# Float64 weights of a Hyena-and-two-MLP kernel: all decoded during the convolution, with four VectorE instructions a job

## The chip, the cores and the metric

One core of one Trainium2 chip runs the whole kernel. The time is device microseconds of one execution. The core has TensorE (PE in the profile, PEld for its weight loads), VectorE (DVE), ScalarE (ACT), GpSimd (POOL) and SyncE (SP, which here only issues DMAs). Three runs of the kernel before have a median of 3026.67 us.

## The reference, cut to what matters

```python
# x, v: (2, 12480, 128); pos_emb: (12480, 64)
h_filt = (np.maximum(pos_emb @ w1, 0.0) @ w2) * np.exp(-0.01 * pos)[:, None]
u = x * v
y = irfft(rfft(u, n=2*S, axis=1) * rfft(h_filt, n=2*S, axis=0), n=2*S, axis=1)[:, :S]
x = (x * y).reshape(24960, 128)
for each of two layers:                      # w_in (128, 2048), w_out (2048, 128), float64
    h = x @ w_in
    g = h if h > 0 else exp(h) - 1           # first layer
    g = h * cos(h)                           # second layer
    x = g @ w_out
```

The four weight matrices arrive as float64, since a float32 array is multiplied there by a float64 scalar. The chip gets them as 64-bit integers and has to make float32 values of them, with all 24 bits of mantissa and a split in two parts: a rounded one (`hi`, float32r) and the rest (`lo`).

## The kernel before, in words

**Filter (0 to about 50 us).** The taps of the filter are computed into `h_all`.

**Convolution (about 50 to 740 us).** 32 chunks of four channels go through a transform in stages: `st_a` (matmuls into `ps_a`, two multiplications by twiddle factors `za` and `zb` on VectorE, their sum `z_t` on POOL), `st_b` (matmuls into `ps_b`, and the product with the filter `ya`, `ps_b`, `y_t` on VectorE, rounded to `yh` on ACT), `lo_y` (`yl = y_t - yh` on POOL), `st_c` (matmuls into `ps_c`, `wa` and `wb` on VectorE, the sum `w_t` on POOL) and `st_d` (matmuls into `ps_d`, `at` on VectorE, a DMA to `xt_d`). `prod` multiplies x and v on POOL (`u_t`). For each chunk `k` is 0 and 1 for the two sequences and 2 for the filter; with k = 2, `st_b` only evacuates, on ACT (`hr`, `hi_f`, lines 360 to 362). The accumulators `ps_a`, `ps_b` and `ps_c` have one buffer each, so the next matmuls into one wait for the VectorE instructions that read it. The order of all this is the list `steps`, written out by hand and run 34 times; one run of the list is called a pass here, and each engine executes its instructions in the order in which the list emits them. All loads of x and v, all stores and the decoder's transfers are on SP's one queue.

**First decoder.** `Decode` is a generator: it emits a few instructions, yields, and is resumed by `next(now, None)` in the loop over `steps`, after every `st_a`, `st_c`, `st_d` and `lo_y` from the second pass on. That makes nine slots a pass. A job takes 256 columns (or rows) of one matrix: `words` (lines 112 to 123) takes the upper and the lower 32-bit words apart, `split` (125 to 145) makes the value `av` and the rest `bv`, `store` (147 to 167) writes `hi` and `lo` to `w_d` in HBM, and for two of the eight blocks of w_out the unsplit value to `wf_d`. Six instructions of a job are VectorE's: `sg`, `mag`, `keep`, `bits`, `av`, `pw`. POOL has `bv`, `dv` and `lo`, ACT has `sq`, `lf` and the copy to `hi`. A job takes nine yields, one more where `wf_d` is written. This generator does the 16 jobs of the first layer.

**Layers (about 740 us to the end).** Each of 52 tiles of 480 tokens per layer runs through eight blocks (`gemm1`, the nonlinearity, a split, `gemm2` five blocks later); line 578 copies the finished tile of the first layer into `x1`.

**Second decoder.** `arena` decodes the second layer's weights during the first layer, in eight jobs of 512 columns, in the part of `x1` that is still free. One `next(later, None)` per block advances it, from block 8 on. Here `dv` and `lo` are VectorE's too (`self.e`), eight VectorE instructions a job. The weights are read back from `w_d` at the end of the first layer (`reload`).

Of the kernel before, what the change touches and what calls it, by code (L numbers as in the profile page):

```python
# [18 lines left out]
B, S, D, FO, DFF = 2, 12480, 128, 64, 2048  # L19
# [10 lines left out]
T = 480  # L30
# [10 lines left out]

DELAY = (1, 2)
DELAY_A = (2, 2)
TINY = float(np.array([897 << 20], np.int32).view(np.float32)[0])


def tables():
# [27 lines left out]
def hyena_moe_kernel(ctx: ExitStack, tc: tile.TileContext, x, v, pe, w1, w2,  # L75
                     wi1, wo1, wi2, wo2, fa, tw, dft, ti, g, win, out):
    nc = tc.nc
# [18 lines left out]
    class Decode:  # L96


        def __init__(self, alloc, n, layer, which, q):
            self.t, self.layer, self.which, self.n = alloc, layer, which, n  # L100
            self.e = nc.vector if layer else nc.gpsimd
            self.o = o = q * n
            w = ((wi1, wo1), (wi2, wo2))[layer][which]
            self.wide = w.dtype != F32
            self.raw = self.t("raw", w.dtype)
            if which == 0:
                nc.sync.dma_start(self.raw, w[:, o:o + n])
            else:
                nc.sync.dma_start(self.raw.rearrange("p (k d) -> p k d", d=128),
                                  w[o:o + n, :].rearrange("(k p) d -> p k d", p=128))  # L110

        def words(self):
            if not self.wide:
                return
            w = self.raw.bitcast(I32).rearrange("p (n w) -> p n w", w=2)
            top, low = w[:, :, 1], w[:, :, 0]
            self.sq, self.lf, self.sg, self.mag = self.t("sq", F32), self.t("lf", F32), self.t("sg", I32), self.t("mag", I32)
            nc.scalar.activation(self.sq, top.bitcast(F32), AF.Square)
            nc.vector.tensor_scalar(self.sg, top, -2147483648, None, op0=ALU.bitwise_and)
            yield  # L120
            nc.scalar.activation(self.lf, low.bitcast(U32), AF.Copy, scale=2.0 ** -52)
            nc.vector.tensor_scalar(self.mag, top, 3, 0x7FFFFFFF, op0=ALU.logical_shift_left, op1=ALU.bitwise_and)
            yield

        def split(self):
            self.hi, self.lo = self.t("hi", F32R), self.t("lo", F32R)
            if not self.wide:
                self.av = self.raw
                copy_r(self.hi, self.raw)
                yield  # L130
                return
            keep, bits, self.av, pw, self.bv = (self.t("keep", I32), self.t("bits", I32), self.t("av", F32),
                                                self.t("pw", I32), self.t("bv", F32))
            nc.vector.tensor_scalar(keep, self.sq, TINY * TINY, -1.0, op0=ALU.is_ge, op1=ALU.mult)
            yield
            nc.vector.scalar_tensor_tensor(bits, self.mag, 0x40000000, self.sg,
                                           op0=ALU.bitwise_xor, op1=ALU.bitwise_or)
            yield
            nc.vector.tensor_tensor(self.av.bitcast(I32), bits, keep, op=ALU.bitwise_and)  # L139
            yield  # L140
            nc.vector.tensor_scalar(pw, self.av.bitcast(I32), -8388608, None, op0=ALU.bitwise_and)
            copy_r(self.hi, self.av)
            yield
            nc.gpsimd.tensor_tensor(self.bv, self.lf, pw.bitcast(F32), op=ALU.mult)
            yield

        def store(self):
            l, wh, n, p = self.layer, self.which, self.n, self.o
            nc.sync.dma_start(w_d[l, wh, 0, :, p:p + n], self.hi.bitcast(F32))
            for m in FULL[l] if wh else ():  # L150
                o = m * 256 - p
                if 0 <= o < n:
                    full = self.av[:, o:o + 256]
                    if self.wide:
                        full = self.t("full", F32)[:, 0:256]
                        nc.gpsimd.tensor_tensor(full, self.av[:, o:o + 256], self.bv[:, o:o + 256], op=ALU.add)
                        yield
                    nc.sync.dma_start(wf_d[l, m], full)
            if self.wide:
                dv = self.t("dv", F32)  # L160
                self.e.tensor_tensor(dv, self.av, self.hi.bitcast(F32), op=ALU.subtract)
                yield
                self.e.tensor_tensor(self.lo, dv, self.bv, op=ALU.add)
            else:
                nc.gpsimd.tensor_tensor(self.lo, self.av, self.hi.bitcast(F32), op=ALU.subtract)
            yield
            nc.sync.dma_start(w_d[l, wh, 1, :, p:p + n], self.lo.bitcast(F32))

        def run(self):
            for part in (self.words, self.split, self.store):  # L170
                yield from part()

    with tc.manual_schedule():
        with ExitStack() as cs:
            taps_ = cs.enter_context(tc.tile_pool(name="taps", bufs=1))
            const = cs.enter_context(tc.tile_pool(name="const", bufs=1))
# [23 lines left out]
            with ExitStack() as fs:  # L200
# [3 lines left out]
                pw = fs.enter_context(tc.tile_pool(name="pw", bufs=1, space=PSUM))  # L204
# [102 lines left out]
            with ExitStack() as vs:  # L307
# [102 lines left out]
                def alloc(name, dt):  # L410
                    return (p2 if name == "raw" else p1).tile([128, 256], dt, name=name, tag=f"d_{name}")

                def first_layer():
                    jobs = [(0, w, q) for w in range(2) for q in range(DFF // 256)]
                    nxt = Decode(alloc, 256, *jobs[0])
                    for i in range(len(jobs)):
                        dec = nxt
                        if i + 1 < len(jobs):
                            nxt = Decode(alloc, 256, *jobs[i + 1])
                        yield from dec.run()  # L420

                now = first_layer()
                prod(0, 0)
                steps = ((st_a, 0, 2), (st_b, 1, 1), (lo_y, 1, 0), (st_d, 2, 1), (prod, 0, 1), (st_a, 0, 0),
                         (lo_y, 1, 1), (prod, -1, 0), (st_c, 1, 0), (st_b, 0, 2), (st_a, 0, 1),
# [1 line left out]
                for p in range(NCH + 2):  # L427
                    for f, back, k in steps:
                        if 0 <= p - back < NCH:
                            f(p - back, k)  # L430
                        if f in (st_a, st_c, st_d, lo_y) and p > 0:
                            next(now, None)
                        if f is prod and back < 0:
                            load(p + 2)
# [149 lines left out]
        def reload(n, wh):  # L584
            l, j, m = blocks[n]
            if l == 0 and j == NTC - 1:
                layers[1].load(nc.sync, wh, m)

        ARENA = T * 20
        ASIZE = (B * S - ARENA) // 2  # L590

        def arena():
            jobs = [(1, w, q) for w in range(2) for q in range(DFF // 512)]
            for i, job in enumerate(jobs):
                free = [ARENA + i % 2 * ASIZE]

                def alloc(name, dt):
                    n = 512 * (2 if name == "raw" and dt != F32 else 1)
                    t = x1[:, free[0]:free[0] + n]
                    free[0] += n  # L600
                    return t if dt == F32 else t.bitcast(dt)

                dec = Decode(alloc, 512, *job)
                for _ in range(4):
                    yield
                yield from dec.run()

        later = arena()
        for wh in range(2):
            for q in range(NBLK):  # L610
                layers[0].load(nc.scalar, wh, q)
# [8 lines left out]
        for n in range(NBK + LAG):  # L620
            if n < NBK:
                l, j, m = blocks[n]
                gemm1(n)
                reload(n, 0)
                if 8 <= n < 200:
                    next(later, None)
                if m == NBLK // 2:
                    nl, nj = (l, j + 1) if j + 1 < NTC else (l + 1, 0)
                    if nl < 2:
                        split_x(nl, nj)  # L630
                    if l == 0:
# [46 lines left out]
```

## Time and profile before

| | us |
|---|---|
| median of three runs | 3026.67 (3023.61 to 3031.22) |
| profiled execution, its own time | 3032.04 |
| span of the profile | 3030.2 |
| granted TensorE clock over the span | 0.993 |

The 1.8 us between the profiled execution's time and its span lie around the program. The profiled execution is 5.4 us above the median of the runs. In the rows below L12 is line 12 of the kernel, `out<-in` are the program's names without buffer numbers (tiles of the arena are all called `x`), and an arrow `<-` behind a wait names what ended it.

### The profile page before, as it was taken

To read this page: it belongs to the slowest core of one execution; us is meant where nothing else is said; L and a number is where in the kernel's file an instruction comes from. 1 tells how busy PE (TensorE), PEld (TensorE's weight loads), DVE (VectorE), ACT (ScalarE), POOL (GpSimd) and SP (SyncE) were. 2 spreads that over 40 slices of the span, in tenths; PEclk is the share of its full clock that TensorE was granted. 3 is DMA by queue.
4 is the path that set the end of the run, shared out by engine and by line. 5 is a ranking of instruction groups with operands and counts; after the bars stand their busy time and mean duration, and the time that the engine had idled before them with its cause. 6 is when DMAs were issued, how large, how long until landed. Compare 5 with 4: busy or idle time off the path is not lost.

```text
span 3030.2 us, 38341 instructions
## 1 busy us (share of the span) xinstructions
PE 2966.4 (98%) x13140; PEld 2317.9 (76%) x13140; DVE 2587.9 (85%) x3272; ACT 2006.6 (66%) x3076; POOL 2575.1 (85%) x1632
## 2 busy tenths in 40 slices
PE   8999999998999999999999999999999999999999
PEld 6777677775777777888888887787888878888887
DVE  5999987876999998888888888788888888888887
ACT  2111111112887888888888888788888888888887
POOL 4888877775898998888888888888888888888888
PEclk9999999998999999999999999999999999999999
DMA  3232322222011100000000001000000000000000
GB/s 103 76 84 78 87 63 64 63 53 88 24 38 38 45 21 10 14 10 14 10 14 11 14 11 40 23 14 10 14 11 13 11 14 10 14 11 14 11 14 14
DMA packets 79635, 96.16 MB, mean 32 GB/s; under 512 B 5722, under 2 KB 63096, under 8 KB 79442
## 3 DMA queue, kind: packets, MB, share of 16 engines
q1 hardware_dynamic: 74016, 88.07, 10.0%
q10 hardware_dynamic: 5426, 5.65, 0.6%
q8 instruction: 105, 1.72, 0.2%
q14 instruction: 88, 0.72, 0.1%
HBM read 59.16 MB, written 34.54 MB: 31 GB/s over the span
## 4 chain that ended last, share of the span: by engine, by line
PE 83%; DVE 12%; issue 2%; ACT 2%; POOL 1%; DMA 0%; POOLq 0%; ACTq 0%; DVEq 0%
PE o_ps L573 34%; PE h_ps L504 32%; PE ps_b L356 6%; PE ps_c L387 4%; PE ps_d L405 2%; PE ps_a L336 2%; DVE e L519 2%; DVE e L521 2%; DVE wb L391 1%; DVE wa L391 1%; DVE ya L368 1%; DVE av L139 1%; ACT e L515 1%; DVE ps_b L369 1%; DVE zb L341 1%
## 5 line engine op out<-in xcount | busy, mean ns | idle before, releaser
L94 POOL TENSOR_TENSOR gl<-e,gh 128x960 fp32r<-128x960 f32 x624 | 1414.7, 2274 | 127.3 <-ACT gh L85 92.6
L504 PE MATMUL h_ps<-xh,w 128*128 128x480 f32 x3328 | 1074.8, 404 | 26.6 <-DVE e L521 22.6
L504 PEld LDWEIGHTS h_ps<-xh,w 128*128 128x128 f32 x3328 | 623.4, 188 | 220.6 <-issue 73.0
L573 PE MATMUL o_ps<-gh,w 128*128 128x480 f32 x2496 | 746.7, 380 | 0.0
L534 DVE SCALAR_TENSOR_TENSOR e<-e,h_ps 128x960 f32<-128x960 int32 x416 | 480.2, 1154 | 201.6 <-ACT e L532 146.9
L504 PE MATMUL h_ps<-xl,w 128*128 128x480 f32 x1664 | 632.8, 380 | 0.1
L519 DVE SCALAR_TENSOR_TENSOR e<-e,t_ps 128x480 f32<-128x480 f32 x832 | 534.4, 651 | 96.2 <-ACT t_ps L517 87.6
L515 ACT ACTIVATE e<-h_ps 128x480 f32<-128x480 f32 x832 | 473.0, 569 | 173.4 <-PE h_ps L504 143.7
L532 ACT ACTIVATE e<-h_ps 128x960 int32<-128x960 f32 x416 | 404.2, 972 | 200.0 <-PE h_ps L504 197.0
L573 PEld LDWEIGHTS o_ps<-gh,w 128*128 128x128 f32 x2496 | 468.9, 188 | 76.1 <-issue 0.8
L93 POOL TENSOR_SCALAR gh<-e 128x960 fp32r<-128x960 f32 x416 | 422.9, 1017 | 114.8 <-DVE e L521 88.9
L517 ACT ACTIVATE t_ps<-h_ps 128x480 f32<-128x480 f32 x832 | 476.4, 573 | 15.6 <-DVE e L519 15.5
L573 PE MATMUL o_ps<-gl,w 128*128 128x480 f32 x1248 | 476.4, 382 | 3.0 <-POOL gl L94 2.9
L541 ACT ACTIVATE e<-e,half_pi 128x960 f32<-128x960 f32 x416 | 453.6, 1090 | 0.3 <-DVE e L534 0.3
L521 DVE SCALAR_TENSOR_TENSOR e<-e,h_ps 128x480 f32<-128x480 f32 x624 | 377.6, 646 | 0.0
L573 PE MATMUL o_ps<-gf,wf 128*128 128x480 f32 x832 | 368.6, 565 | 0.0
L543 DVE TENSOR_TENSOR e<-e,h_ps 128x960 f32<-128x960 f32 x312 | 358.1, 1148 | 1.3 <-ACT e L541 1.2
L504 PEld LDWEIGHTS h_ps<-xl,w 128*128 128x128 f32 x1664 | 313.0, 188 | 53.3 <-POOL xl L94 0.8
L85 ACT ACTIVATE yh<-y_t 128x720 fp32r<-128x720 f32 x64 | 51.5, 805 | 411.2 <-DVE y_t L371 335.9
L573 PEld LDWEIGHTS o_ps<-gl,w 128*128 128x128 f32 x1248 | 234.7, 188 | 42.3 <-POOL gl L94 5.0
L356 PE MATMUL ps_b<-z_t,dft_t 128*128 128x360 f32 x768 | 254.3, 475 | 8.8 <-DVE y_t L371 8.2
L344 POOL TENSOR_TENSOR z_t<-za,zb 128x720 f32<-128x720 f32 x96 | 141.9, 1478 | 114.2 <-DVE zb L341 114.2
(94 smaller groups left out, 3479.0 us busy)
## 6 DMA issues: line engine op xcount, KB each, us to landing
x_t<-in_x SPq DMA_DIRECT2D x32, 392.0 KB
v_t<-in_v SPq DMA_DIRECT2D x32, 392.0 KB
xt_d<-at SPq DMA_DIRECT2D x64, 196.0 KB
out<-ot SPq DMA_DIRECT2D x52, 240.0 KB
x_in<-xt_d SPq DMA_DIRECT2D x50, 240.0 KB
w_d<-x SPq DMA_DIRECT2D x16, 256.0 KB
w<-w_d ACTq DMA_DIRECT2D x14, 256.0 KB
w<-w_d SPq DMA_DIRECT2D x14, 256.0 KB
```

Source lines behind the costliest of these rows:

```text
L93: ENG[plan[0]].tensor_scalar(hi, full, 1.0, 0.0, op0=ALU.mult, op1=ALU.add)
L94: ENG[plan[1]].tensor_tensor(lo, full, hi.bitcast(F32), op=ALU.subtract)
L356: nc.tensor.matmul(ps[:, r, 0:n], dft_t[:, sl], z[:, q], start=j == 0, stop=j == 1)
L504: nc.tensor.matmul(h[:, 0:T], a, b, start=k == 0, stop=k == 2)
L515: nc.scalar.activation(u[:, e], hs[e][:, 0:T], AF.Exp)
L517: nc.scalar.activation(ts[e][:, 0:T], hs[e][:, 0:T], AF.Tanh, scale=0.5)
L519: nc.vector.scalar_tensor_tensor(u[:, e], u[:, e], 1.0, ts[e][:, 0:T], op0=ALU.add, op1=ALU.mult)
L521: nc.vector.scalar_tensor_tensor(gt[:, e], u[:, e], 0.0, hs[e][:, 0:T], op0=ALU.min, op1=ALU.max)
L532: nc.scalar.activation(kq, hv, AF.Copy, scale=1.0 / TWO_PI, bias=0.25)
L534: nc.vector.scalar_tensor_tensor(rr, kq, -TWO_PI, hv, op0=ALU.mult, op1=ALU.add)
L541: nc.scalar.activation(rr, rr, AF.Sin, bias=half_pi)
L573: nc.tensor.matmul(o, a, b[:, e], start=f == 0 and k == 0, stop=f == NFT - 1 and k == len(mm) - 1)
```

## The change

Both layers' weights are decoded by the one generator in the convolution: 32 jobs of 256 columns. Three more slots are used, behind the three `st_a` of the first pass. The arena is gone. A job has another sequence: `sq` is turned in place by ACT's Sign into an integer mask (-1 or +1), `mag` is built in three VectorE instructions in place (the last of them applies the mask), `pw` is a scalar_tensor_tensor, POOL multiplies `lf` by `pw` in place and adds it to `mag` as `full`, ACT rounds `full` to `hi`, and POOL subtracts for `lo`. `dv`, `bv`, `keep`, `sg`, `bits` and `av` are gone, and `wf_d` is stored from `full`. A job takes eight yields.

```diff
         def words(self):
...
-            self.sq, self.lf, self.sg, self.mag = self.t("sq", F32), self.t("lf", F32), self.t("sg", I32), self.t("mag", I32)
+            self.sq, self.lf, self.mag = self.t("sq", F32), self.t("lf", F32), self.t("mag", I32)
             nc.scalar.activation(self.sq, top.bitcast(F32), AF.Square)
-            nc.vector.tensor_scalar(self.sg, top, -2147483648, None, op0=ALU.bitwise_and)
+            nc.vector.tensor_scalar(self.mag, top, 0x0FFFFFFF, 3, op0=ALU.bitwise_and, op1=ALU.logical_shift_left)
+            yield
+
+            self.keep = self.sq.bitcast(I32)
+            nc.scalar.activation(self.keep, self.sq, AF.Sign, scale=-1.0, bias=below)
+            nc.vector.scalar_tensor_tensor(self.mag, top, -2147483648, self.mag,
+                                           op0=ALU.bitwise_and, op1=ALU.bitwise_or)
             yield
             nc.scalar.activation(self.lf, low.bitcast(U32), AF.Copy, scale=2.0 ** -52)
-            nc.vector.tensor_scalar(self.mag, top, 3, 0x7FFFFFFF, op0=ALU.logical_shift_left, op1=ALU.bitwise_and)
-            yield
...
-            nc.vector.tensor_scalar(keep, self.sq, TINY * TINY, -1.0, op0=ALU.is_ge, op1=ALU.mult)
-            yield
-            nc.vector.scalar_tensor_tensor(bits, self.mag, 0x40000000, self.sg,
-                                           op0=ALU.bitwise_xor, op1=ALU.bitwise_or)
-            yield
-            nc.vector.tensor_tensor(self.av.bitcast(I32), bits, keep, op=ALU.bitwise_and)
-            yield
-            nc.vector.tensor_scalar(pw, self.av.bitcast(I32), -8388608, None, op0=ALU.bitwise_and)
-            copy_r(self.hi, self.av)
-            yield
-            nc.gpsimd.tensor_tensor(self.bv, self.lf, pw.bitcast(F32), op=ALU.mult)
-            yield
+            av, pw, self.full = self.mag.bitcast(F32), self.t("pw", I32), self.t("full", F32)
+            nc.vector.scalar_tensor_tensor(self.mag, self.mag, 0x40000000, self.keep,
+                                           op0=ALU.bitwise_xor, op1=ALU.bitwise_and)
+            yield
+            nc.vector.scalar_tensor_tensor(pw, self.mag, -8388608, self.mag, op0=ALU.bitwise_and, op1=ALU.bitwise_and)
+            yield
+            nc.gpsimd.tensor_tensor(self.lf, self.lf, pw.bitcast(F32), op=ALU.mult)
+            yield
+            nc.gpsimd.tensor_tensor(self.full, av, self.lf, op=ALU.add)
+            yield
+            copy_r(self.hi, self.full)
+            yield
...
-                    nc.sync.dma_start(wf_d[l, m], full)
-            if self.wide:
-                dv = self.t("dv", F32)
-                self.e.tensor_tensor(dv, self.av, self.hi.bitcast(F32), op=ALU.subtract)
-                yield
-                self.e.tensor_tensor(self.lo, dv, self.bv, op=ALU.add)
-            else:
-                nc.gpsimd.tensor_tensor(self.lo, self.av, self.hi.bitcast(F32), op=ALU.subtract)
+                    nc.sync.dma_start(wf_d[l, m], self.full[:, o:o + 256])
+            nc.gpsimd.tensor_tensor(self.lo, self.full, self.hi.bitcast(F32), op=ALU.subtract)
             yield
...
-                def first_layer():
-                    jobs = [(0, w, q) for w in range(2) for q in range(DFF // 256)]
+                def decode():
+                    jobs = [(l, w, q) for l in range(2) for w in range(2) for q in range(DFF // 256)]
...
-                        if f in (st_a, st_c, st_d, lo_y) and p > 0:
+                        if f in (st_a, st_c, st_d, lo_y) and (p > 0 or f is st_a):
                             next(now, None)
...
-        later = arena()
...
-                if 8 <= n < 200:
-                    next(later, None)
```

## Rows read from the trace of the kernel before

**Rows 1.** The page, busy us, share of the span and instructions by engine.
```profile
PE 2966.4 (98%) x13140; PEld 2317.9 (76%) x13140; DVE 2587.9 (85%) x3272; ACT 2006.6 (66%) x3076; POOL 2575.1 (85%) x1632
```

**Rows 2.** By stretch, per engine: busy us (instructions); then PE clock, DMA share, GB/s.
```profile
101.79:271.63 169.84, 163.61 (x835) 121.20 (x833) 157.32 (x193) 31.00 (x66) 140.41 (x97) 1.00 0.30 82
444.66:606.57 161.91, 161.91 (x834) 121.48 (x833) 129.23 (x144) 22.45 (x41) 120.01 (x73) 1.00 0.23 60
780.26:1086.13 305.87, 288.89 (x1195) 220.74 (x1194) 301.50 (x480) 248.74 (x479) 273.62 (x165) 1.00 0.12 38
1107.67:1409.28 301.61, 301.61 (x1289) 241.77 (x1288) 269.10 (x449) 253.67 (x492) 269.27 (x169) 1.00 0.05 12
```

**Rows 3.** Line 362 in four stretches: durations, first and last start (us).
```profile
L362 ACT ACTIVATE hi_f<-ps_b x9: 478/478/478, 101.8 to 271.6; 128x360 f32<-128x360 f32 x9
...
L362 ACT ACTIVATE hi_f<-ps_b x3: 478/479/479, 380.1 to 424.4; 128x360 f32<-128x360 f32 x3
...
L362 ACT ACTIVATE hi_f<-ps_b x17: 472/478/479, 80.5 to 424.4; 128x360 f32<-128x360 f32 x17
...
L362 ACT ACTIVATE hi_f<-ps_b x15: 478/478/479, 424.4 to 707.8; 128x360 f32<-128x360 f32 x15
```

**Rows 4.** Line 578 in two stretches: durations, first and last start (us).
```profile
L578 ACT ACTIVATE x<-o_ps x14: 571/574/577, 780.3 to 1086.1; 128x480 f32<-128x480 f32 x14
...
L578 ACT ACTIVATE x<-o_ps x15: 570/572/573, 1107.7 to 1409.3; 128x480 f32<-128x480 f32 x15
```

**Rows 5.** Timeline, VectorE and POOL: start us, duration us, engine, line, instruction [idle before].
```profile
70.84 0.28 DVE L119 TENSOR_SCALAR sg<-raw 128x256 int32<-128x256 int32 x1
...
119.84 0.41 DVE L136 SCALAR_TENSOR_TENSOR bits<-mag,sg 128x256 int32<-128x256 int32 x1
120.36 1.50 DVE L139 TENSOR_TENSOR av<-bits,keep 128x256 int32<-128x256 int32 x1
...
120.06 1.51 POOL L344 TENSOR_TENSOR z_t<-za,zb 128x720 f32<-128x720 f32 x1 [1.93 <-DVE zb L341]
...
382.46 2.45 DVE L139 TENSOR_TENSOR av<-bits,keep 128x256 int32<-128x256 int32 x1
...
383.17 1.46 POOL L344 TENSOR_TENSOR z_t<-za,zb 128x720 f32<-128x720 f32 x1
```

**Rows 6.** Groups of instructions, shapes apart: count, busy us, mean ns, idle before.
```profile
L139 DVE TENSOR_TENSOR av<-bits,keep 128x256 int32<-128x256 int32 x16 | 25.3, 1583 | 1.1
...
L134 DVE TENSOR_SCALAR keep<-sq 128x256 int32<-128x256 f32 x16 | 12.1, 758 | 0.0
...
L144 POOL TENSOR_TENSOR bv<-lf,pw 128x256 f32<-128x256 f32 x16 | 11.7, 730 | 0.0
...
L118 ACT ACTIVATE sq<-raw 128x256 f32<-128x256 f32 x16 | 6.8, 425 | 0.0
```

**Rows 7.** Waits (total us, times, longest): PE early, PE late, VectorE without decoding.
```profile
PE ps_c L387 <- DVE wb L391: 6.2, 8, 0.8
...
PE ps_b L356 <- DVE y_t L371: 4.9, 5, 1.4
...
PEld ps_c L387 <- POOL yl L328: 3.7, 8, 0.5
...
DVE wa L391 <- PE ps_c L387: 16.3, 16, 1.1
DVE za L341 <- POOL u_t L317: 10.3, 8, 1.3
DVE ya L368 <- PE ps_b L356: 4.9, 8, 0.6
```

**Rows 8.** Timeline of a pass without decoding, POOL, then PE.
```profile
517.69 1.72 POOL L328 TENSOR_TENSOR yl<-y_t,yh 128x720 fp32r<-128x720 f32 x1
...
519.68 0.28 PE L387 MATMUL ps_c<-dft_h,yl 128*90 128x256 f32 x1
```

**Rows 9.** Timeline of the first pass, VectorE.
```profile
63.37 0.91 DVE L341 TENSOR_TENSOR za<-ps_a,tw_t 128x720 f32<-128x720 f32 x1 [4.04 <-PE ps_a L336]
```

More of the change, by code (lines that the diff above doesn't have):

```diff
@@ L43 @@
 DELAY_A = (2, 2)
-TINY = float(np.array([897 << 20], np.int32).view(np.float32)[0])
+TINY = np.array([897 << 20], np.int32).view(np.float32)[0]
+BELOW = float(np.nextafter(TINY * TINY, np.float32(0)))
 def tables():
@@ L100, in __init__ @@
             self.t, self.layer, self.which, self.n = alloc, layer, which, n
-            self.e = nc.vector if layer else nc.gpsimd
             self.o = o = q * n
@@ L127, in split @@
             if not self.wide:
-                self.av = self.raw
+                self.full = self.raw
                 copy_r(self.hi, self.raw)
@@ L131, in split @@
                 return
-            keep, bits, self.av, pw, self.bv = (self.t("keep", I32), self.t("bits", I32), self.t("av", F32),
-                                                self.t("pw", I32), self.t("bv", F32))
-            nc.vector.tensor_scalar(keep, self.sq, TINY * TINY, -1.0, op0=ALU.is_ge, op1=ALU.mult)
+            av, pw, self.full = self.mag.bitcast(F32), self.t("pw", I32), self.t("full", F32)
+            nc.vector.scalar_tensor_tensor(self.mag, self.mag, 0x40000000, self.keep,
+                                           op0=ALU.bitwise_xor, op1=ALU.bitwise_and)
             yield
-            nc.vector.scalar_tensor_tensor(bits, self.mag, 0x40000000, self.sg,
-                                           op0=ALU.bitwise_xor, op1=ALU.bitwise_or)
+            nc.vector.scalar_tensor_tensor(pw, self.mag, -8388608, self.mag, op0=ALU.bitwise_and, op1=ALU.bitwise_and)
             yield
-            nc.vector.tensor_tensor(self.av.bitcast(I32), bits, keep, op=ALU.bitwise_and)
+            nc.gpsimd.tensor_tensor(self.lf, self.lf, pw.bitcast(F32), op=ALU.mult)
             yield
-            nc.vector.tensor_scalar(pw, self.av.bitcast(I32), -8388608, None, op0=ALU.bitwise_and)
-            copy_r(self.hi, self.av)
+            nc.gpsimd.tensor_tensor(self.full, av, self.lf, op=ALU.add)
             yield
-            nc.gpsimd.tensor_tensor(self.bv, self.lf, pw.bitcast(F32), op=ALU.mult)
+            copy_r(self.hi, self.full)
             yield
@@ L152, in store @@
                 if 0 <= o < n:
-                    full = self.av[:, o:o + 256]
-                    if self.wide:
-                        full = self.t("full", F32)[:, 0:256]
-                        nc.gpsimd.tensor_tensor(full, self.av[:, o:o + 256], self.bv[:, o:o + 256], op=ALU.add)
-                        yield
-                    nc.sync.dma_start(wf_d[l, m], full)
-            if self.wide:
-                dv = self.t("dv", F32)
-                self.e.tensor_tensor(dv, self.av, self.hi.bitcast(F32), op=ALU.subtract)
-                yield
-                self.e.tensor_tensor(self.lo, dv, self.bv, op=ALU.add)
-            else:
-                nc.gpsimd.tensor_tensor(self.lo, self.av, self.hi.bitcast(F32), op=ALU.subtract)
+                    nc.sync.dma_start(wf_d[l, m], self.full[:, o:o + 256])
+            nc.gpsimd.tensor_tensor(self.lo, self.full, self.hi.bitcast(F32), op=ALU.subtract)
             yield
@@ L171, in run @@
                 yield from part()
+    one = ctx.enter_context(tc.tile_pool(name="one", bufs=1))
+    below = one.tile([128, 1], F32, name="below")
     with tc.manual_schedule():
+        nc.vector.memset(below, BELOW)
         with ExitStack() as cs:
@@ L420, in first_layer @@
                         yield from dec.run()
-                now = first_layer()
+                now = decode()
                 prod(0, 0)
@@ L587, in reload @@
                 layers[1].load(nc.sync, wh, m)
[L589 to L604, printed above, removed]
-                    yield
-                yield from dec.run()
-        later = arena()
         for wh in range(2):
```

## The prediction

> **What bounds the kernel now.** I read the engine totals first: PE is busy for 98% of the span [rows 1], so time can only be won in stretches where PE waits. The table by stretch shows where these are [rows 2]. In a convolution stretch without decoding (444.66 to 606.57 us) PE is busy for all 161.91 us; in one with decoding (101.79 to 271.63) for 163.61 of 169.84. In the first layer PE is busy for 288.89 of 305.87 us while second-layer weights are decoded, and for all of 301.61 us afterwards. So both decoders cost time, and nothing else in these stretches does.
>
> How much they cost is read from a regular event. One evacuation of line 362 runs per pass of the convolution [rows 3]: without decoding 14 passes take 707.8 - 424.4 = 283.4 us, 20.24 each. The 16 passes with decoding take 343.9 us where 16 x 20.24 = 323.8 were enough: **20.1 us** is the price of the first-layer decoder. It is not even: 21.23 us a pass from 101.8 to 271.6 (+0.98), 22.15 from 380.1 to 424.4 (+1.9). In between, each of the two jobs with a wf_d store takes one slot more, and the jobs behind it start one slot later. One copy of line 578 runs per token tile [rows 4]: 13 tiles with decoding take 305.8 us, 14 later ones 301.6, or 21.54 each. 305.8 - 13 x 21.54 = **25.8 us** is the price of the second-layer decoder.
>
> Why it costs, I read from the timeline. `bits` starts while POOL stands still and takes 0.41 us; `av`, just behind it, starts inside POOL's z_t and takes 1.50 us, ending 0.29 us after z_t does; a later `av`, in the slot behind st_a(1), takes 2.45 us and again ends 0.28 us after a z_t [rows 5]. The means of the groups mix such cases: 0.76 us for `keep`, a tensor_scalar like `sg` with its 0.28, and 1.58 for `av` [rows 5, 6]. A VectorE instruction that reads two SBUF operands, or one in the decoder's tensor_scalar form, stands still here until POOL's current instruction ends, and all of VectorE's queue with it. [...] What goes late is the evacuation of PSUM: PE waits for wb in the early passes (101.79 to 271.63 us), and for y_t, which frees ps_b, in the late ones (314.56 to 424.41) [rows 7].
>
> **The change, part by part.** The decoder advances one yield at a slot; there are nine slots a pass, after st_a(2), lo_y(0), st_d(1), st_a(0), lo_y(1), st_c(0), st_a(1), st_c(1) and st_d(0). I call them A2, Y0, D1, A0, Y1, C0, A1, C1, D0.
>
> *Arena removed.* 64 VectorE instructions, 24 ACT and 10 POOL instructions leave the first layer, with eight raw loads and 18 stores on SP. What remains of tiles 1 to 13 is the work of the later tiles, so -25.8 us. The least it can be is PE's own idle time, 305.87 - 288.89 = 17.0 [rows 2]; I take the tile count, since it also holds matmuls stretched by late operands. Nothing is late next: the later tiles have PE full.
>
> *Old first-layer decoder removed:* -20.1 us.
>
> *New decoder.* A job takes 8 yields (three with an instruction each of VectorE and ACT, one with VectorE alone, two with POOL, one with ACT, one with POOL). 32 jobs need 256 slots; three lie in the first pass, so 253 / 9 = 28.1 passes. It ends before the convolution does. A job of 8 in a ring of 9 drifts by one slot per pass, so all four VectorE instructions visit every slot; the old one stood still for ten jobs.
>
> VectorE's part: 4 x 32 = 128 instructions in place of 6 x 16 = 96. Unblocked, a job would cost 0.28 + 3 x 0.41 = 1.5 us [rows 5], and VectorE idles 16.3 + 10.3 + 4.9 = 31.5 us over eight passes without decoding, 3.9 each [rows 7]; so it is the blocking, not the sum, that counts. I price an instruction at what the old ones cost on average, 20.1 / 96 = 0.21 us: 128 x 0.21 = **+26.8 us**, 0.95 a pass. By slots it comes out alike. The early passes' 0.98 belongs to the pair A0 and Y1, where the second instruction is caught behind z_t [rows 5]; three of the eight drift patterns fill both. Four put an instruction at C1, directly ahead of ya, ps_b and y_t, the queue for which PE waits in the late passes; three of these also hold A1, where the `av` of 2.45 us stood. At 0.98 for the first kind, 1.4 for those three (under the late passes' 1.9, as they hold five or four instructions, not six) and 0.4 for the other two, the mean is (2.9 + 4.2 + 0.8) / 8 = 0.99.
> The ends: only the three pairs cost anything, 3/8 x 0.98 = 0.37 a pass, 10 us in all; or every pass is like the late ones, 1.9 a pass, 54 us.
>
> POOL's part: three instructions a job (`lf`, `full`, `lo`) as before (`bv`, `dv`, `lo`), 0.73 us each [rows 6]. POOL idles (161.91 - 120.01) / 8 = 5.2 us a pass without decoding [rows 2], so the 46 more lie beside other work, except at A2, ahead of yl(0): yl ends at 519.41 and its first matmul is at 519.68 [rows 8], so one there makes PE late by 0.73 - 0.27 = 0.46. Three of eight patterns have it, 0.17 a pass; the late passes show waits for yl too, so I take this as held in the 0.95. Without that cover it is 4.9 us.
>
> ACT's part: one `Sign` more a job, 16 more jobs. ACT is busy for 22.45 of 161.91 us [rows 2]: nothing, or, all of it exposed, 32 x 0.43 us [rows 6], 14 us. The wait that it adds: the copy to `hi` now waits for POOL's `full`, and hr, hi_f and yh stand behind it in ACT's queue. It comes one slot later than `full`; only at C0, just ahead of hr, does it bite, one pattern in eight, up to 0.5 us.
>
> SP's part: 16 more raw loads and 34 more stores, among x, v and xt_d transfers. The loads are issued a pass ahead: nothing. First pass: the first instruction on VectorE waits for the first raw load; VectorE idles for 4.04 us in this pass [rows 9], so between 0 and 4 us; I take 0.
>
> Sum: -25.8 - 20.1 + 26.8 = **-19 us**. The profiled execution took 3032.04 us, so 3013; the median of the runs is 5.4 lower, and on it the forecast is 3026.7 - 19 = **3008 us**.
>
> **A rule that gives another time.** On durations alone (0.28 and 0.41 us unblocked [rows 5]) the new job's 1.5 us disappears in 3.9 us of idle time, and the convolution would keep almost no excess: -25.8 - 20.1 = -46, 2981. That is the limit of the first rival. [...]
>
> **Rivals.** (1) *Most blocking is hidden*: below 0.5 us a pass. For it: an instruction that follows zb starts before z_t does, as `bits` did, and each gap in front of wa holds one of these. Against: `av` was blocked every time. At 0.37 a pass, 10 us: -36, 2991. Chance 0.17. (2) *A draw*: 1.3 to 1.95 a pass, the drift finding A1 and C1 as costly as the late passes did; at 1.5, 42 us, -4: 3023. Chance 0.14. (3) *Slower*: at C1 and D0 each delay of VectorE moves y_t, hence ps_b, and z_t(2), behind which POOL's decoder instruction stands before yl; both waits add up in every pass. The late passes' 1.9 plus 0.3 is 2.2 a pass, 62 us: +16, 3043. It decides from 45.9 / 28.1 = 1.63 a pass. Against: four to five VectorE instructions in a pass, not six. Chance 0.05. (4) *The first layer stays slow*, because something other than the arena holds it: -20.1 + 26.8 = +7, 3033. Against: VectorE's busy time falls from 301.50 of 305.87 to 269.10 of 301.61 us when the arena ends, and PE's idle time to none [rows 2]. Chance 0.03.
>
> **Numbers.** Forecast (0.5 to 1.3 a pass, -32 to -9 us) 0.61. 0.3% of this time is 9 us, about what can be told from no change. Faster by more: forecast and (1), 0.78. Within: most of (2), (4) and the forecast's edge, 0.16. Slower: (3) and a tip of (2), 0.06. The range takes in (1) down to 0.37 a pass and (2) up to 1.45: 2991 to 3022.
>
> **What would show it.** Right: token tiles 1 to 13 at 21.5 us with no wait of PE for e or gf; passes with decoding between 20.7 and 21.5 us, uneven with a period of eight; PE waits for wb in some and for y_t or yl in others; the new VectorE instructions with means of 0.6 to 1.0 us, longest where z_t or w_t runs. Wrong: passes of 20.3 us (rival 1), passes of 22 us throughout (2, 3), first tiles that stay at 23 us (4), or ACT with yh and hr late behind `hi`.

## The result: 0.6% slower

The changed kernel takes 3045.23 us, the median of 4 runs (3043.72 to 3046.16), beside 3026.53 for the kernel before: a ratio of 1.006, interval 1.0042 to 1.0077. The forecast was 3008, 2991 to 3022. The sign was wrong; the time is that of the third rival (3043), which had a chance of 0.05. The profiled execution of after took 3043.72 us.

The engine totals of after, on its page, answer to [rows 1]: PE is still busy for almost all of the span, and that total hides where the time went.

```profile
PE 2962.8 (97%) x13140; PEld 2324.2 (76%) x13140; DVE 2593.0 (85%) x3241; ACT 2025.1 (67%) x3132; POOL 2585.6 (85%) x1668
```

The table by stretch of after: eight consecutive passes of the convolution, each from one st_a(2) to the next, then 14 token tiles of the first layer. The columns are those of [rows 2].

```profile
265.26:289.50 24.24, 20.69 (x106) 15.13 (x105) 23.89 (x24) 4.37 (x9) 17.38 (x13) 1.00 0.28 77
289.50:316.25 26.75, 22.21 (x106) 16.66 (x104) 25.48 (x24) 4.27 (x9) 18.38 (x13) 0.94 0.25 65
316.25:336.95 20.70, 20.45 (x106) 15.15 (x104) 19.20 (x23) 4.39 (x9) 19.09 (x14) 1.00 0.32 84
336.95:358.95 22.00, 20.68 (x106) 15.14 (x104) 19.55 (x23) 4.69 (x10) 18.07 (x14) 1.00 0.32 86
358.95:379.27 20.32, 20.32 (x105) 15.17 (x104) 16.05 (x22) 4.28 (x9) 15.96 (x13) 1.00 0.32 93
379.27:401.68 22.41, 20.57 (x106) 15.20 (x105) 17.89 (x24) 4.60 (x10) 17.99 (x14) 1.00 0.29 78
401.68:423.55 21.87, 20.48 (x105) 15.18 (x104) 20.03 (x25) 4.79 (x10) 18.04 (x13) 1.00 0.35 94
423.55:444.86 21.31, 20.44 (x106) 15.16 (x105) 19.61 (x24) 4.59 (x10) 17.21 (x13) 1.00 0.29 86
819.68:1121.28 301.60, 301.60 (x1289) 241.77 (x1288) 269.24 (x449) 253.59 (x491) 269.08 (x169) 1.00 0.05 12
```

The last row is the first layer without its decoder: PE busy for all of it from the first copy of line 573 (line 578 before) on, 14 tiles in 301.60 us, 21.54 each. The stretch that took 305.87 for 13 tiles [rows 2, 4] is gone. The eight passes above it are the loss. They repeat with a period of eight, as a job of 8 yields in a ring of nine must, and their mean is 22.45 us against 20.24 without decoding. Two of them, 24.24 and 26.75, hold 10.5 of the 17.7 us of this period's excess.

The evacuation of line 357 answers to [rows 3]; the columns of this view of one line are count, durations (ns) and first and last start (us).

```profile
L357 ACT ACTIVATE hi_f<-ps_b x29: 474/477/478, 78.2 to 709.5; 128x360 f32<-128x360 f32 x29
```

28 passes take 709.5 - 78.2 = 631.3 us; 28 x 20.24 = 566.7 were enough. So the new decoder costs **64.6 us**, 2.31 a pass, where 0.95 was forecast. At the first copy of the second product after stands 39.4 us behind before (819.68 against 780.26); it wins 25.8 back over tiles 1 to 13, and some 1.5 at the change of layers, and is about 12 behind from there on. The profiled executions differ by 11.7 us and the medians by 18.7, since the profiled one of before was 5.5 above its median and that of after 1.5 below.

The groups of the decoder's own instructions in after, columns as in [rows 6]:

```profile
L120 DVE TENSOR_SCALAR mag<-raw 128x256 int32<-128x256 int32 x32 | 53.2, 1663 | 0.0
L125 DVE SCALAR_TENSOR_TENSOR mag<-raw,mag 128x256 int32<-128x256 int32 x32 | 27.0, 842 | 0.1
L138 DVE SCALAR_TENSOR_TENSOR mag<-mag,sq 128x256 int32<-128x256 int32 x32 | 26.4, 824 | 1.6 <-ACT sq L124 1.2
L141 DVE SCALAR_TENSOR_TENSOR pw<-mag 128x256 int32<-128x256 int32 x32 | 30.0, 939 | 0.1
L145 POOL TENSOR_TENSOR full<-mag,lf 128x256 f32<-128x256 f32 x32 | 23.4, 731 | 0.6
```

Four VectorE instructions of a job take (53.2 + 27.0 + 26.4 + 30.0) / 32 = 4.27 us. The six of before took 74.9 / 16 = 4.68. A third of the instructions went and hardly any of the time. The first mag, 0.28 us by itself, has a mean of 1.66. The timeline of the 24.24 us pass, VectorE, then POOL, then PE's next matmul into ps_c (columns as in [rows 5]), shows the worst of them:

```profile
274.49 0.90 DVE L336 TENSOR_TENSOR zb<-ps_a,tw_t 128x720 f32<-128x720 f32 x1
275.31 4.77 DVE L120 TENSOR_SCALAR mag<-raw 128x256 int32<-128x256 int32 x1
280.00 1.21 DVE L386 TENSOR_TENSOR wa<-ps_c,ti_t 90x1024 f32<-90x1024 f32 x1
...
274.15 0.75 POOL L145 TENSOR_TENSOR full<-mag,lf 128x256 f32<-128x256 f32 x1
274.85 1.31 POOL L312 TENSOR_TENSOR u_t<-x_t,v_t 98x512 f32<-98x512 f32 x1
276.09 1.49 POOL L339 TENSOR_TENSOR z_t<-za,zb 128x720 f32<-128x720 f32 x1
277.52 0.75 POOL L157 TENSOR_TENSOR lo<-full,hi 128x256 fp32r<-128x256 f32 x1
278.20 1.73 POOL L323 TENSOR_TENSOR yl<-y_t,yh 128x720 fp32r<-128x720 f32 x1
279.87 1.35 POOL L312 TENSOR_TENSOR u_t<-x_t,v_t 98x512 f32<-98x512 f32 x1
...
282.49 0.32 PE L382 MATMUL ps_c<-dft_h,yh 128*90 128x256 f32 x1 [1.79 <-DVE wb L386]
```

This mag is issued right behind zb, at the same place as the sg and bits that ran at once in [rows 5]. There POOL stood waiting for zb. Here `full` has pushed u_t back, u_t still runs when zb ends, and z_t, lo and yl follow it with no gap. Mag stands for 4.77 us, through four POOL instructions, and ends 0.15 us after yl does. wa starts right behind it, and PE waits 1.79 us for wb in this pass.

The waits of after in the whole convolution, 80 to 712 us; columns are the total in us, times, and longest:

```profile
PE ps_c L382 <- DVE wb L386: 23.6, 15, 3.1
PE ps_b L351 <- DVE y_t L366: 18.1, 16, 1.4
DVE wa L386 <- POOL w_t L393: 20.6, 10, 3.4
PE ps_c L382 <- POOL yl L323: 6.7, 15, 0.6
PEld ps_c L382 <- ACT hi_f L357: 3.2, 5, 1.3
```

PE waits for wb and y_t, as in [rows 7]; in the same stretch of before it was 8.8 and 4.9 us. New is VectorE's own wait for w_t, of which before has none in that stretch.

### The profile page after: what moved, and what is told of

It is laid out like the page before. It is cut to its first block, busy times and chain, and to the rows that moved or that the text cites. A ratio compares the mean times of both kernels' runs of the same rounds, so it can differ in the third digit from the quotient of the medians.

```text
span 3041.9 us, 38471 instructions
## 1 busy us (share of the span) xinstructions
PE 2962.8 (97%) x13140; PEld 2324.2 (76%) x13140; DVE 2593.0 (85%) x3241; ACT 2025.1 (67%) x3132; POOL 2585.6 (85%) x1668
## 4 chain that ended last, share of the span: by engine, by line
PE 84%; DVE 10%; issue 2%; POOL 2%; ACT 0%; DMA 0%; POOLq 0%; ACTq 0%; SPq 0%; DVEq 0%
PE o_ps L568 38%; PE h_ps L499 36%; PE ps_b L351 4%; PE ps_c L382 3%; DVE mag L120 1%; PE ps_a L331 1%; DVE wb L386 1%; PE ps_d L400 1%; DVE ya L363 1%; DVE ps_b L364 1%; DVE wa L386 1%; DVE zb L336 1%; DVE y_t L366 1%; DVE za L336 1%; PE h_ps L269 1%
## 5 line engine op out<-in xcount | busy, mean ns | idle before, releaser
L514 DVE SCALAR_TENSOR_TENSOR e<-e,t_ps 128x480 f32<-128x480 f32 x832 | 543.6, 654 | 121.9 <-ACT t_ps L512 110.8
L95 POOL TENSOR_SCALAR gh<-e 128x960 fp32r<-128x960 f32 x416 | 414.8, 997 | 118.8 <-DVE e L516 97.0
L568 PEld LDWEIGHTS o_ps<-gf,wf 128*128 128x128 f32 x832 | 157.0, 189 | 100.8 <-issue 88.6
```

Source lines behind the costliest of these rows:

```text
L95: ENG[plan[0]].tensor_scalar(hi, full, 1.0, 0.0, op0=ALU.mult, op1=ALU.add)
L514: nc.vector.scalar_tensor_tensor(u[:, e], u[:, e], 1.0, ts[e][:, 0:T], op0=ALU.add, op1=ALU.mult)
L568: nc.tensor.matmul(o, a, b[:, e], start=f == 0 and k == 0, stop=f == NFT - 1 and k == len(mm) - 1)
```

## The experiments

The explanations that stood against each other: the form of the instructions (A; the first mag is a tensor_scalar), the slot that VectorE's instructions fall on (B, later V), the single buffers of wa and wb (C), and POOL's instructions, which now wander through the row u_t, z_t, yl (P). Where no ratio stands beside a time below, it is that of one execution; the kernel before took 3025 to 3029 us beside these.

**Form, and buffers of wa and wb (e1, e2).** e1 changes one instruction, e2 one pool.

```
-            nc.vector.tensor_scalar(self.mag, top, 0x0FFFFFFF, 3, op0=ALU.bitwise_and, op1=ALU.logical_shift_left)
+            nc.vector.scalar_tensor_tensor(self.mag, top, 0x0FFFFFFF, three, op0=ALU.bitwise_and, op1=ALU.logical_shift_left)
```
```
-                    t1 = p1.tile([NF, DC * n], F32, name="wa")
+                    t1 = p2.tile([NF, DC * n], F32, name="wa")
```

> The first mag instruction of a job, a tensor_scalar that took 4.4 to 4.8 us behind st_a(0) and lo_y(1), becomes a scalar_tensor_tensor with a constant tile of threes; nothing else changes. Theory A (the tensor_scalar form is held off by a closed row of POOL instructions, a two-input form only by one or two of them): mag falls to 2.5 us or less in these slots, the two worst passes from +4.1 and +4.6 to about +2, and the kernel to about 3028 us. Rival B (it is the slot, whatever the form): mag stays at 4.4 to 4.8 us there and the time at 3045 within 3 us.

> The tiles wa and wb get two buffers each, so that wa of st_c(1) no longer waits until POOL's w_t of st_c(0) has read the old ones; nothing else changes. Theory C (POOL's decoder instructions, queued ahead of w_t, stop VectorE through the single buffers; 19.9 us of VectorE's idle time before wa carries this name): 3027 to 3037 us, and that wait is gone. Theory A or B alone (the loss is in the blocked mag): 3042 us or more.

e1: 3049.80 us, beside 3026.20 of the kernel before. Its group of line 120:

```profile
L120 DVE SCALAR_TENSOR_TENSOR mag<-raw,three 128x256 int32<-128x256 int32 x32 | 57.3, 1790 | 0.0
```

The form is not it: the mean stays (1790 ns for 1663), and at the same two slots mag stands for 4.9 and 4.5 us. e2 (wb likewise): 3040.55 us, between the two expectations. VectorE's wait for w_t is gone. The passes of 22.4 and 21.9 fall to 21.2 and 20.9; those of 24 to 27 stay. So this wait costs some 5 us (28 passes take 626.8 us for 631.4) and is not the main cause of the loss.

**The slot of a job, and the move alone (e3, e4).** e3 lets a job take nine slots, moving on one slot after every third; e4 keeps the old six-instruction decoder (with dv and lo on POOL), moves all its jobs into the convolution and drops the arena.

```
                         yield from dec.run()
+                        yield
+                        if i % 3 == 2 and i < 27:
+                            yield
```
```
-                    jobs = [(0, w, q) for w in range(2) for q in range(DFF // 256)]
+                    jobs = [(l, w, q) for l in range(2) for w in range(2) for q in range(DFF // 256)]
```

> A job takes nine slots in place of eight (one empty yield), so it stands still in the pass, and every third job an extra empty yield moves it on by one slot: three jobs at each of the nine places. If the drift itself is what costs (a place costs little once the engines have settled): the second and third pass at each place under 21.2 us, and the kernel at 3028 or less. If single places cost (the mag instruction behind st_a(0) and lo_y(1)): passes of 23.5 to 25 us at these two places and 20.3 to 21.5 elsewhere, about 3038 us in all.

> The decoder of before, six VectorE instructions a job, decodes both layers in the convolution (32 jobs, arena removed): the move without the new instructions. The jobs behind the first layer's last stand where the late passes had them. If a VectorE instruction costs what it cost before (0.21 us, 1.9 us a pass in the late places): 20 + 16 x 1.9 = 50 us of excess in the convolution, 27 us saved behind it, 3030 us. If any second half of decoding costs what the changed kernel shows (2.3 us a pass): 32 x 2.3 = 74, 3053 us.

e3: 3045.50 us, above both expectations, though it is single places that cost, as the second one had it. By the slot of the first mag the passes take 21.6 us (A2), 21.4 (Y0), 20.8 (D1), 21.7 (A0), 23.8 (Y1), 24.0 (C0), 23.8 (A1), 21.2 (C1) and 22.4 (D0). At A0 mag takes 0.28 us, at Y1 4.37, so the same slot A0 that held it for 4.38 us in the changed kernel lets it through at once here: a slot has no price of its own, it depends on what POOL holds at that moment. e4: 3038.39 us, between the expected 3030 and 3053. Its first jobs stand as in before (21.2 us a pass), the later ones in the place of the late passes of [rows 3], 22.2 us a pass, and the last passes rise to 24.1 and 26.1. So the move alone, at the old instructions, already costs about 12 us net, and the four-instruction job, which wanders, is about 7 us dearer still than six that mostly stand.

**Placing the pieces (e5 to e8).** From here each piece of a job has its slot, by a table in place of the chain of yields; VectorE's four are d1 to d4, POOL's product, sum and low half are m, a and l, ACT's copy to `hi` is h. A2 is slot 0 and D0 slot 8, from 9 on it is the next pass, and a job starts every nine slots. The table of e5, and then those of e6, e7 and e8:

```
+                PLACES = [(2, 'd1'), (3, 'd2'), (4, 'd3'), (5, 'd4'), (6, 'm'), (7, 'a'), (8, 'h'), (9, 'l'), (10, 's')]
...
-                        yield from dec.run()
+                    todo = sorted((9 * i + at, i, k, piece) for i in range(len(jobs))
+                                  for k, (at, piece) in enumerate(PLACES))
+                    for t in range(todo[-1][0] + 1):
+                        while todo and todo[0][0] == t:
+                            _, i, _, piece = todo.pop(0)
...
+                            decs[i].piece(piece)
+                        yield
```
```
+                PLACES = [(4, 'd1'), (5, 'd2'), (6, 'd3'), (7, 'd4'), (8, 'm'), (8, 'a'), (9, 'h'), (17, 'l'), (17, 's')]
+                PLACES = [(2, 'd1'), (3, 'd2'), (4, 'd3'), (5, 'd4'), (9, 'm'), (10, 'a'), (11, 'h'), (12, 'l'), (13, 's')]
+                PLACES = [(0, 'd1'), (1, 'd2'), (3, 'd3'), (5, 'd4'), (8, 'm'), (8, 'a'), (9, 'h'), (17, 'l'), (17, 's')]
```

> The changed kernel's job stands still at the cheapest of the nine places of the run with empty yields: VectorE's four instructions behind st_d(1), st_a(0), lo_y(1) and st_c(0), POOL's behind st_a(1), st_c(1) and, in the next pass, st_a(2). One job a pass, from the second pass on. There such passes took 20.75 us: 32 x 0.5 = 16 us of excess in place of about 65. Every theory: 2995 to 3000 us, faster than both kernels. If a standing job is no better than a drifting one over 32 passes: 3035 or more.

> VectorE's four instructions stand at one of the dearest places (behind lo_y(1), st_c(0), st_a(1), st_c(1): 23.8 us a pass and mag at 4.4 us when POOL's three stood at st_d(0), st_a(2) and st_d(1)), but POOL's three go behind st_d(0), where POOL idles. Theory P (POOL's decoder instructions late in the pass close up its row of u_t, z_t, yl, u_t, and VectorE is held off until the row has a gap): mag at 1.6 us or less there, passes of 21.6 or less, 3023 us or less. Theory V (the place of VectorE's instructions decides): mag at 4.4, passes of 23.8, about 3095 us.

> The reverse: VectorE's four instructions at the cheapest place, as in the standing kernel, but POOL's three behind st_a(2), lo_y(0) and st_a(0), inside the row. Theory P: passes of 22.5 us or more, the instruction behind st_a(0) or lo_y(1) held for 2.5 us or more, 3050 us or more. Theory V: 20.75 a pass, 2995 to 3002 us.

> VectorE's four instructions one by one at four places with idle time ahead of the next stage (behind st_a(2), lo_y(0), st_a(0), st_c(0)), POOL's three behind st_d(0). Theory P: no closed row and no pair, passes of 20.5 us or less, 2990 us or less. Theory V (the sum over these places from the run with empty yields): 20.7 to 21.2, 2996 to 3012 us.

e5: 3000.12 us, ratio 0.9906 (0.9889 to 0.9922), its passes at 20.7 to 20.9. e6: 3064.72. Its first mag stands at Y1 as in the timeline of after, with POOL's pieces gone to D0; VectorE's row, then POOL's around it:

```profile
279.87 0.28 DVE L119 TENSOR_SCALAR mag<-raw 128x256 int32<-128x256 int32 x1
...
286.17 2.77 DVE L128 SCALAR_TENSOR_TENSOR mag<-mag,sq 128x256 int32<-128x256 int32 x1
...
276.00 1.71 POOL L311 TENSOR_TENSOR yl<-y_t,yh 128x720 fp32r<-128x720 f32 x1
280.10 1.47 POOL L327 TENSOR_TENSOR z_t<-za,zb 128x720 f32<-128x720 f32 x1 [1.13 <-DVE zb L324]
```

POOL waits for zb again, and mag takes 0.28 us in place of 4.77. But the third instruction, at A1, takes 2.77 in two passes in a row (from 264.26 and from 286.17 us), and PE, idle for 1.65 us in most passes (21.91 - 20.26), waits for y_t (18 times from 200 to 600 us, 26.8 us in all, 1.7 at the longest), so VectorE's late places have a price of their own. Neither theory had this run right: P's mag came true and its time (3023) didn't, and V's mag and time (3095) both failed. Two passes in a row of e6, by stretch, show one more thing:

```profile
291.23:313.14 21.91, 20.26 (x106) 15.19 (x105) 19.73 (x23) 4.38 (x9) 17.59 (x12) 1.00 0.27 80
313.14:336.74 23.60, 21.95 (x106) 16.03 (x105) 19.73 (x23) 4.38 (x9) 17.56 (x12) 0.93 0.26 74
```

VectorE and POOL do the same work for the same time. In the second, PE's granted clock is 0.93 over the pass in place of 1.00, PE is busy 1.7 us longer (21.95 for 20.26), and the pass is 1.7 us longer. 15 passes of e6 are like this (0.93), 5 of after (0.93 or 0.94; the one of 26.75 us is one), the 3 dear ones of e8 below (0.93), none of before's passes with decoding (1.00). In after's pass of 26.75 us the clock is 0.50, half level, from 309.0 to 312.0 us, and a matmul into ps_c takes 0.42 us there in place of 0.28.

e7: 3076.48 us. VectorE is as in e5, POOL's pieces lie at A2, Y0 and A0; the pass goes from 20.7 to 23.1. Its waits, 80 to 650 us:

```profile
DVE wa L374 <- POOL w_t L381: 47.4, 25, 2.0
PE ps_c L370 <- DVE wb L374: 38.2, 25, 1.6
DVE mag L119 <- POOL full L138: 20.3, 24, 1.1
```

So POOL's three short instructions, in that row, cost 2.4 us a pass, though VectorE's four decoder instructions took only 3.4 us a pass together (546.61 / 28 = 19.52 us of VectorE in a pass, less the 16.15 of a pass without decoding [rows 2]); with three of them at their unblocked 0.28, 0.41 and 0.41, the fourth averaged 2.3 us at most (theory P had 2.5 or more). POOL's three also make w_t late, and VectorE waits for its buffers. Some 0.8 us a pass VectorE waits at mag for `full`, since mag has one buffer; how much of the 2.4 that is was not separated. e8: 3006.47 us, ratio 0.9926 (0.9911 to 0.9941): 20.37 a pass, but three of 24, at each of which POOL's sum waits for the transfer of the `full` before (two such waits from 200 to 600 us, 5.3 us in all), and a longer end. The passes are those of theory P (20.5 or less), the time is in V's range and not P's (2990 or less).

**POOL's place alone (e9), its control (e11), and the best version (e10).** e9 is e3 with POOL's pieces put at D0 (ACT's h at the next A2), two buffers for sq, mag, lf, pw and full, and jobs from the first pass's first slot on; e11 is the changed kernel with those buffers alone; e10 is e8 with the edits of the third block.

```
+                        first = 9 * i + min(i, 26) // 3
+                        m = (first + 3) // 9 * 9 + 8
+                        todo += [(first + k, i, k, f"d{k + 1}") for k in range(4)]
+                        todo += [(m, i, 5, "m"), (m, i, 6, "a"), (m + 1, i, 7, "h"), (m + 9, i, -2, "l"), (m + 9, i, -1, "s")]
```
```
-                    return (p2 if name == "raw" else p1).tile([128, 256], dt, name=name, tag=f"d_{name}")
+                    return (p2 if name in ("raw", "mag", "lf", "pw", "sq", "full") else p1).tile([128, 256], dt, name=name, tag=f"d_{name}")
```
```
-                        if f in (st_a, st_c, st_d, lo_y) and p > 0:
+                        if f in (st_a, st_c, st_d, lo_y):
...
-                    t1 = p1.tile([NF, DC * n], F32, name="wa")
-                    t2 = p1.tile([NF, DC * n], F32, name="wb")
+                    t1 = p2.tile([NF, DC * n], F32, name="wa")
+                    t2 = p2.tile([NF, DC * n], F32, name="wb")
...
-                    return (p2 if name == "raw" else p1).tile([128, 256], dt, name=name, tag=f"d_{name}")
+                    return (p2 if name in ("raw", "full") else p1).tile([128, 256], dt, name=name, tag=f"d_{name}")
```

> VectorE's four instructions wander through the slots as in e3 (nine slots a job and one more after every third), but POOL's product and sum of every job are put at slot D0, its rounded half's copy at the next A2 and the low half at the next D0; mag, lf, pw, sq and full have two buffers. In e3 the passes went by the slot of d1: 21.55, 21.37, 20.75, 21.7, 23.8, 24.0, 23.8, 21.2, 22.4 us for A2 to D0, a mean of 22.3, with half-level stretches at Y1's and its neighbours' places. Theory P (it is POOL's wandering instructions, in the row from A2 to Y1, that hold VectorE up and make w_t late): the mean falls to some 21.1; places A2 to A0 give 20.4 to 20.9 as in e8, C0 to C1 at most 21.9 as in e6's passes at full clock, the first mag at Y1 takes under 1 us, and the kernel comes to 3005 to 3018 us. Theory V (it is VectorE's own late places, wherever POOL's stand): passes of 23 us and more stay at C0 to A1, and the kernel stays over 3035 us.

> e8 with what its trace left: full, wa and wb have two buffers (e8: three passes of 23.9 to 24.1 us in place of 20.37, at each of them POOL's full waiting for the transfer of the one before; wa waiting 1.4 us a pass for w_t), and all nine slots of pass 0 are used too, so that the last job ends a pass earlier (e8's first copy of the second product stands at 784.98 against 775.10 in e5, though its passes were shorter). If e8's convolution is bounded by what is left of VectorE's price: the three passes give 11 us back, the end 10, and the 31 passes up to 0.1 each: 2982 to 2990 us. If the waits named are only where other lateness shows, the three passes stay at 24 and the time over 2998.

> The changed kernel with one line other: the decoder's sq, mag, lf, pw and full have two buffers, as e9 gave them; everything wanders as in the changed kernel. e9 differs from e3 in POOL's places and in these buffers, and this tells the two apart. If the place was it (theory P): the 4.4 and 4.8 us at Y1's and A0's slots and the passes of 24 to 27 us stay, and the kernel stays at 3038 to 3048 us (changed kernel 3045). If the buffers were it: those passes fall to 21 to 22, and the kernel comes to 3012 to 3022 us.

28 passes, from the third st_a(2) on, by stretch: e3, then e9.

```profile
85.70:706.64 620.94, 581.84 (x2913) 430.08 (x2912) 539.02 (x613) 118.56 (x248) 485.01 (x333) 0.98 0.28 79
```
```profile
86.47:680.28 593.81, 571.48 (x2914) 424.80 (x2912) 528.39 (x613) 119.98 (x248) 491.45 (x334) 1.00 0.29 82
```

e9: 3012.77 us, as theory P had it. The same instructions, with POOL's in one place, take 27.1 us less: 16.8 of PE's idle time (39.1 to 22.3) and 10.4 of its busy time, most of it in the six passes of e3 with a granted clock of 0.93 (PE busy for 21.86 to 21.97 us in each, beside 20.41 in the mean of e9's); e9 has none of these. What stays is 593.81 - 566.7 = 27.1 us, 0.97 a pass. Its dear passes (21.4 to 21.9) are those with the first mag at Y0 and from A0 to A1, but for the first one at A0 (20.45), and the first at C1; theory P had Y0 and A0 among the cheap ones. The first mag at Y1 takes 0.28; at A1 it takes 2.1. e11: 3044.43 us, with 4.78 and 4.39 us for mag at the old places, and its 28 passes take 631.4 us as in the changed kernel; the buffers alone do nothing, so the place did it (ACT's h moved with it and was not tried by itself).

e10: **2982.70 us**, ratio 0.9857 (0.984 to 0.9873). Its 28 passes, and its decoder's groups:

```profile
87.19:656.03 568.84, 567.34 (x2913) 425.42 (x2912) 501.91 (x617) 119.84 (x252) 494.52 (x337) 1.00 0.31 87
```
```profile
L119 DVE TENSOR_SCALAR mag<-raw 128x256 int32<-128x256 int32 x32 | 9.0, 283 | 0.0
L123 DVE SCALAR_TENSOR_TENSOR mag<-raw,mag 128x256 int32<-128x256 int32 x32 | 15.2, 474 | 0.0
L128 DVE SCALAR_TENSOR_TENSOR mag<-mag,sq 128x256 int32<-128x256 int32 x32 | 13.3, 416 | 0.0
L132 DVE SCALAR_TENSOR_TENSOR pw<-mag 128x256 int32<-128x256 int32 x32 | 32.2, 1008 | 0.0
```

PE is busy for all but 1.5 of 568.84 us, 20.32 a pass. The same four instructions and three of POOL, with two buffers for wa, wb and full, cost 2.1 us in all 28 passes here and 64.6 in the changed kernel.

## Why the prediction was wrong, point by point

*Arena removed, -25.8: right.* 21.54 us a tile from the first on, with PE full. *Old decoder removed, -20.1: right* as a baseline: the cheapest pass of after takes 20.32.

*VectorE's part, +26.8 at 0.21 us an instruction: this step failed.* Measured, by the same division, are 64.6 / 128 = 0.50. The price was the mean of instructions that stood in one place for ten jobs, with POOL's decoder instructions standing still as well. The forecast named the pair A0 and Y1 as the dear one and gave it 0.98 a pass; the passes in which the first mag stands at Y1 and A0 cost 4.0 and 6.5. Nor does VectorE's time tell it: the decoder takes 4.27 us of it a job, less than the 4.68 of before, and a pass costs 2.31 in place of 1.26. A ring makes some passes dear and some cheap, and the cheap ones give nothing back, since with PE full 20.2 to 20.3 us is the least that a pass of the convolution took in these runs. Of the signs named in advance, the period of eight and PE's waits for wb and y_t came; the passes run from 20.3 to 26.8 us in place of 20.7 to 21.5, and the first mag's mean is 1.66 us in place of 0.6 to 1.0.

*POOL's part, "the 46 more lie beside other work, except at A2": this is the assumption that broke the price.* The forecast looked at what a POOL instruction delays on POOL, and found idle time of 5.2 us a pass to put it in. It didn't look at what that idle time does: part of it is the gap, behind zb, in which VectorE's decoder instruction gets in. e3 against e9 prices POOL's wandering at 27 us of 54, at nine and a third slots a job; with it gone, what is left comes to 0.97 a pass, beside the forecast's 0.95 to 0.99 for VectorE's part. That the two agree is partly luck: 15 of e9's 28 passes lie 1.1 to 1.7 us above 20.24, where the forecast gave 0.98 to the pair A0 and Y1 and 1.4 to the places with C1 and A1. For the changed kernel's own eight slots the split between POOL's wandering and VectorE's places was not measured.

*How long VectorE stands.* The prediction read a wait until POOL's current instruction ends. Its own second `av` [rows 5] already stood longer: when it starts, at 382.46 us, z_t has not begun, and POOL still has this to finish (before, columns as in [rows 5]):

```profile
380.59 2.63 POOL L398 TENSOR_TENSOR w_t<-wa,wb 90x1024 f32<-90x1024 f32 x1
```

So that av stood through the end of w_t and all of z_t, and the first mag of after through four POOL instructions, 4.77 us. A POOL row without a gap isn't enough to explain it. In another pass of after the third instruction of a job is held by z_t alone, and gets in when z_t ends, though yl follows z_t without a gap:

```profile
326.03 1.50 DVE L138 SCALAR_TENSOR_TENSOR mag<-mag,sq 128x256 int32<-128x256 int32 x1
...
325.60 1.64 POOL L339 TENSOR_TENSOR z_t<-za,zb 128x720 f32<-128x720 f32 x1
327.20 1.90 POOL L323 TENSOR_TENSOR yl<-y_t,yh 128x720 fp32r<-128x720 f32 x1
```

What decides at which change of POOL's instruction VectorE gets in isn't shown. The traces show that VectorE's decoder instructions stand still, and that the wait can go on through instructions that POOL starts later (2.45 us for that av, 4.77 for mag). Not all of VectorE's work does this: za and zb, which read ps_a, took 0.89 to 0.91 us in every case in before, where `keep` took 0.28 to 1.55 and `av` 1.28 to 2.46. Unblocked, a scalar_tensor_tensor took 0.40 to 0.42 us here (lines 125 and 138 of after, from the least to the median).

*ACT's part, nothing: right.* The copy to `hi` waits long for `full` (77.6 us in all from 80 to 712 us), but the waits of that stretch show no matmul of PE, and no instruction of VectorE or POOL but the decoder's own, that waits for ACT. PE's weight load waits 3.2 us for hi_f there, 11.5 before; the view of line 357 alone gives it 19.2 us, so that this is less sure than the matmuls. *SP's part, nothing:* no wait of after points against it; it wasn't tried by itself.

*Rival 3* had the right size, 2.2 a pass, from another working: the late passes' price in every pass. What it had right is that a POOL instruction ahead of yl counts; PE's waits for yl are 6.7 us, though, and those for wb 23.6. Its chance of 0.05 was too small, since the decision point, 1.63 a pass, lies below the 1.9 that the late passes of before showed; e4, in whose second half nearly every pass is like those, is slower than before too. *The rule on durations alone*, -46 and 2981 us, is what e10 reached (2982.7), by placing and a second buffer for three tiles, and not by the instructions' number.

**Open:** how much of the lower clock is due to which wait of PE was not separated; in e6 PE is idle for 1.64 us or more in 15 passes with a granted clock of 0.93 and in ten others with 1.00.

## What to carry to other kernels

Where VectorE's instructions stand behind POOL's, as here, an instruction's price is not its duration, nor the mean of others like it; it depends on what POOL is doing when it is issued: the same tensor_scalar took 0.28 us in one pass of after and 4.77 in another. Put it right behind the instruction that POOL is waiting for (behind zb it took 0.28 us in e6 and e10), and keep POOL's optional work out of that stretch. Filler that advances by a counter out of step with the loop visits every place, the worst one too; give each piece its slot. In a loop whose cheap passes already have the bounding engine full, price the dear passes one by one, since the cheap ones don't make up for them.

## What the runs showed of the hardware beyond what was expected

A VectorE tensor_scalar of 0.28 us stood for 4.77 us through four POOL instructions in a row; as a scalar_tensor_tensor it stood for 4.90 in the same place (e1; 1.79 us in the mean of 32, for 1.66). PE's granted clock fell to 0.93 or 0.94 over a pass in 5 passes of after and 15 of e6 (in after's pass of 26.75 us to 0.50, half level, from 309.0 to 312.0 us). In each of after's five PE waits once for wb for 1.76 to 3.12 us, in each of e6's 15 it is idle for 1.64 us or more, and in the two passes of e6 shown above PE's work took 1.7 us longer in the second (21.95 for 20.26), with the work of VectorE and POOL the same. Not every such wait came with it: the passes of after from 265.26 and from 470.64 us hold waits of 1.79 and 3.11 us at a clock of 1.00, and e9 has waits for y_t of up to 1.7 and 1.00 in every one of the 28 passes.
